# Sparse attention and a mixture of experts on one core: wider local turns, a strided unit moved ahead, more filler products, one store on another queue

## The chip, the cores and the metric

One Trainium2 chip, one NeuronCore of it. The metric is the device time of one execution in microseconds; lower is better. The engines are TensorE (PE for products, PEld for the load of their stationary operand), VectorE (DVE), ScalarE (ACT), GpSimd (POOL) and SyncE (SP), whose queue issues most transfers.

## The reference

Four batches, eight heads, 576 positions, 64 channels, float32. Heads 0 to 3 attend to the last 32 positions ("local"), heads 4 to 7 to earlier positions of the same remainder modulo 32 ("strided"). The result, 2304 rows of 512, goes through a mixture of 8 experts with one expert for each row.

```python
mask_local = (rel >= 0) & (rel < stride)                       # stride = 32
mask_strided = (rel >= 0) & (pos[None, :] % stride == pos[:, None] % stride)
scores = np.where(masks, scale * q @ k.T, -1e9)
attn_out = softmax(scores) @ v
x = attn_out.transpose(0, 2, 1, 3).reshape(B * S, H * D)
logits = x @ w_gate
expert_idx = np.argmax(logits, axis=1)
# rows go to their expert while it has room (576 rows)
out[i] = gate_w[i] * (np.maximum(x[i] @ w1[e], 0) @ w2[e])
```

## The kernel before

Attention is cut into 16 strided units (`z`) and 9 local ones (`l`). A strided unit is a pair of heads of one batch and half of its position groups; a local unit is 256 rows of the result for the four local heads. Each unit goes through five stages: A turns q and k (they come with positions on the partitions and are needed with channels there), B makes scores, C turns the weights after exp, D multiplies by v, E turns the result for the gate and stores it to `x_dram`. The string `SEQ` is the order of the units, and a loop over its places i runs C(i), A(i+3), B(i+2), E(i-1), exp, D(i): so each engine's program interleaves five units. A turn is a TensorE product with the identity `ident` into one of three PSUM buffers of `ps_t` (tag "t"), from where ScalarE copies it out.

For local units stage A is `l_a(c, nm)`, once for k and once for q of each of 8 head pairs c. `la_target` spreads these 16 calls over the places ahead of the unit that needs them; for batch 0 they start at place `LS`. GpSimd reorders their source first (`l_r`). `fill(t)` is a product of the all-ones tile `hot` (bf16) written into a PSUM tile that the next turn overwrites: it computes nothing that is used. `warm(n)` is n such products of 512 columns.

Loads are issued on SyncE's queue by `put_to` and `put_more`, in the order of their need, a fixed look-ahead in front of the place (`LOOK`), and as far as buffers are free. The queue works in order, and the stores to `x_dram` of stage E go through it as well. The first of all are q and k of the first head pair (`load_z(0, 2)`), then v (`load_zv`) into the buffers `VZ`, whose rows 32 to 63 VectorE sets to zero beforehand.

Behind the last unit, VectorE works out ranks and the first expert; SyncE reads the first expert's number and loads its first weights (`load_w`, twice 512 KB); GpSimd gathers that expert's rows out of `x_dram` (`gather_tile`, three tiles, indices `idx`), TensorE turns them (`x_steps`), and `experts` runs all eight experts (line 1063 is the first product, lines 1052 to 1054 the others). The gathers need every row of `x_dram`, so they wait for the last store too: that of unit `vv == 8` in `l_e`.

Of the kernel before, what the change touches and what calls it, by code (L numbers as in the profile page):

```python
# [9 lines left out]
F32 = mybir.dt.float32  # L10
# [10 lines left out]
STRIDE = 32  # L21
FL = "abgi"
LOOK = 8
SEQ = "zzzzlzzlzzlzzlzzlzzlzzlll"
WARM2 = 4
WA = 2
WB = 6
# [5 lines left out]
NZ = 3  # L33
NL = 3
NV = 3
LS = 3
WARM = 14
SETS = (
# [7 lines left out]
def bc(ap, axis, n):  # L46

    a = ap.unsqueeze(axis)
    shape = list(a.shape)
    shape[axis] = n  # L50
    return a.to_broadcast(shape)
# [3 lines left out]
def kernel(  # L55
# [10 lines left out]
    nc = tc.nc  # L66
# [25 lines left out]
    ident = const.tile([128, 128], F32, name="ident")  # L92
# [22 lines left out]
    def gather_tile(idx, r, xg_p):  # L115
        t = xg_p.tile([128, DM], F32, tag="xg", name="xg")
        nc.gpsimd.indirect_dma_start(  # L117
            out=t[:r], out_offset=None, in_=x_dram[:, :],
            in_offset=bass.IndirectOffsetOnAxis(ap=idx[:r], axis=0),
        )  # L120
        return t, r


    with ExitStack() as p1:
# [5 lines left out]
        ps_t = p1.enter_context(tc.tile_pool(name="ps_t", bufs=3, space=PSUM))  # L130
# [20 lines left out]
        def fill(t):  # L151

            w = t.shape[1]
            nc.tensor.matmul(t, lhsT=hot, rhs=bc(hot[:, 0:w // 4], 1, 4), start=True, stop=True)

        V0S = [cp.tile([128, 16, 65], F32, name=f"v0s{i}") for i in range(NV)]
        VZ = [cp.tile([128, 16, 64], F32, name=f"vz{i}") for i in range(2)]
        V0L = [cp.tile([128, 18, 65], F32, name=f"v0l{i}") for i in range(4)]
        KTL = [cp.tile([128, 32 + S], F32, name=f"ktl{i}") for i in range(4)]
        QTL = [cp.tile([128, S], F32, name=f"qtl{i}") for i in range(4)]  # L160
# [30 lines left out]
        def load_zv(c):  # L191
            b, pair = divmod(c, 2)
            h0 = 4 + 2 * pair
            for h in range(2):
                nc.sync.dma_start(
                    out=VZ[c % 2][64 * h:64 * h + 36],
                    in_=v[b, h0 + h].rearrange("(m g) d -> m g d", g=16),
                )

        def copy_zv(c):  # L200
            nc.gpsimd.tensor_copy(V0S[c % NV][0:100, :, 0:64], VZ[c % 2][0:100])

        def copy_lv(c):
            vt = V0L[c % 4]
            for h in range(2):
                nc.gpsimd.tensor_copy(vt[64 * h:64 * h + 32, 1:18, 0:64], vt[64 * h + 32:64 * h + 64, 0:17, 0:64])  # L206
# [9 lines left out]
        def load_lv(c):  # L216
            b, pair = divmod(c, 2)
            h0 = 2 * pair
            vt = V0L[c % 4]
            for h in range(2):  # L220
# [2 lines left out]
        load_z(0, 2)  # L223
        for i in range(NV):
            nc.gpsimd.memset(V0S[i][:, :, 64], 1.0)
        for i in range(2):
            nc.vector.memset(VZ[i][32:64], 0.0)
        for t in PS:
            nc.gpsimd.memset(t, 0.0)
        for i in range(4):  # L230
            nc.gpsimd.memset(KTL[i][:, 0:32], 0.0)
            nc.gpsimd.memset(V0L[i][:, :, 64], 1.0)
            for h in range(2):
                nc.gpsimd.memset(V0L[i][64 * h:64 * h + 32, 0, 0:64], 0.0)

# [72 lines left out]
        def zid(u):  # L308
            c, gh = divmod(u, 2)
            b, pair = divmod(c, 2)  # L310
            return b, pair, gh, c

        def z_a(u):
            b, pair, gh, c = zid(u)
            for src, nm in ((zk[c], "k"), (zq[c], "q")):
                t = ps_t.tile([128, 4, 72], F32, tag="t", name="tq")
                if nm == "q":
                    fill(t.rearrange("p a b -> p (a b)"))
                for i in range(4):
                    g, h = divmod(i, 2)  # L320
                    g = 4 * gh + 2 * g
                    nc.tensor.transpose(t[:, i, :], src[:, h, g:g + 2, :].rearrange("p g d -> p (g d)"), ident[:72, :72])
                st = wk.tile([128, 4, 72], F32, tag=nm + "t", name=nm + "t")
                nc.scalar.copy(st, t)
                (kts if nm == "k" else qts)[u] = st
# [86 lines left out]
        def l_a(c, nm):  # L412
            src = lr.pop((c, nm))
            dst = QTL[c % 4] if nm == "q" else KTL[c % 4][:, 32:32 + S]
            for p0, p1 in ((0, 64), (64, 96)):
                n = p1 - p0
                t = ps_t.tile([128, 6, n], F32, tag="t", name="tl")
                if p0 == 0:
                    fill(t.rearrange("p a b -> p (a b)"))
                for g in range(6):  # L420
                    nc.tensor.transpose(t[:, g, :], src[p0:p1, g].rearrange("p h d -> p (h d)"), ident[p0:p1, p0:p1])
                nc.scalar.copy(dst[:, 6 * p0:6 * p1].rearrange("d (p g) -> d p g", g=6), t.rearrange("d g p -> d p g"))

        def l_b(vv):
            s = ps_s.tile([128, 2, 512], F32, tag="s", name="sl")
# [24 lines left out]
        def l_c(vv):  # L450
            p = Pl.pop(vv)
            t = ps_t.tile([128, 4, 128], F32, tag="t", name="tpl")
            for i in range(4):
                nc.tensor.transpose(t[:, i, :], p[:, i].rearrange("p h k -> p (h k)"), ident)
            pt = wk.tile([128, 4, 128], F32, tag="pt", name="ptl", bufs=2)
            nc.scalar.copy(pt, t)
            PTl[vv] = pt

        def l_d(vv):
            pt = PTl.pop(vv)  # L460
            o = ps_o.tile([128, 2, 512], F32, tag="o", name="ol")
            for t in range(2):
                for pair in range(2):
                    i = 2 * t + pair
                    for c in range(4):
                        b, blk = divmod(4 * (2 * vv + t) + c, 18)
                        n = (2 * b + pair) % 4
                        for h in range(2):
                            nc.tensor.matmul(
                                o[32 * c:32 * c + 32, h, 65 * i:65 * i + 65],  # L470
                                lhsT=pt[64 * h:64 * h + 64, i, 32 * c:32 * c + 32],
                                rhs=V0L[n][64 * h:64 * h + 64, blk, :],
                                start=True, stop=True,
# [8 lines left out]

        def l_e(vv):
            x = Xl.pop(vv)
            nc.sync.dma_start(
                out=x_dram[256 * vv:256 * vv + 256, 0:256].rearrange("(t p) c -> p t c", p=128),
                in_=x.rearrange("p (t a) h d -> p t (a h d)", t=2),
            )
            t = ps_t.tile([128, 4, 128], F32, tag="t", name="txl")
            for i in range(4):  # L490
                nc.tensor.transpose(t[:, i, :], x[:, i].rearrange("p h d -> p (h d)"), ident)
            xt = wk.tile([128, 4, 128], F32, tag="xtl", name="xtl", bufs=4)
            nc.scalar.copy(xt, t)
            xtl[vv] = xt
# [202 lines left out]
        zu, lu = list(range(16)), list(range(9))  # L697
        for c in SEQ:
            seq.append(("z", zu.pop(0)) if c == "z" else ("l", lu.pop(0)))
        at = {x: i for i, x in enumerate(seq)}  # L700
        n = len(seq)
# [3 lines left out]
        def last_l(b):  # L705
            return (18 * (b + 1) - 1) // 8

        def emit_la(m):
            while la_done[0] < m:
                c, part = divmod(la_done[0], 2)  # L710
                assert c < 4 or done["B", "l"] > last_l((c - 4) // 2)
                put_to("lr", c)
                l_a(c, "kq"[part])
                la_done[0] += 1
# [4 lines left out]
        def la_target(i):  # L719
# [3 lines left out]
            for b in range(B):  # L723
                s0 = first[b - 1] + 1 if b == 1 else (at["l", last_l(b - 2)] + 2 if b > 1 else LS)
                s1 = first[b]
# [56 lines left out]
        def stage(st, i):  # L782
            if not 0 <= i < n:
                return
            kind, u = seq[i]
            if st == "A":
                if kind == "z":
                    put_to("zq", u // 2)
                    z_a(u)
                emit_la(l_need(u) if kind == "l" else la_target(i))  # L790
            elif st == "B":
                (z_b if kind == "z" else l_b)(u)
            elif st == "C":
                (z_c if kind == "z" else l_c)(u)
            elif st == "D":
                if kind == "z":
                    put_to("zc", u // 2)
                else:
                    put_to("lc", 2 * min((8 * u + 7) // 18, B - 1) + 1)
                (z_d if kind == "z" else l_d)(u)  # L800
            elif st == "E":
                (z_e if kind == "z" else l_e)(u)
            done[st, kind] += 1
# [82 lines left out]
        g0 = [gather_tile(idx[0], 128, xg_p)]  # L886
# [112 lines left out]
    with ExitStack() as p2:  # L999
        p0 = p2.enter_context(ExitStack())  # L1000
# [181 lines left out]
        t = pools["ps_w"].tile([128, 512], F32, tag="w", name="warm2")  # L1182
# [133 lines left out]
```

## Time and profile before

| what | value |
|---|---|
| median of 3 runs | 420.32 us (419.13 to 426.94) |
| profiled execution, its own time | 416.89 us |
| its span | 415.1 us |
| TensorE busy (products) | 376.1 us, 91% |
| mean granted TensorE clock | 0.884 |
| attention, from the first turn to the last unit's scores for the gate | 6.6 to about 153 us |
| first product of the experts | 174.47 us |

A granted clock of 1.00 in the profile is 2.4 GHz and one of 0.50 is 1.2 GHz. The timeline names an instruction, its start, its length, and in brackets how long its engine stood idle before it and what ended that.

### The profile page before, as it was taken

Reading aid. Unit: us, or ns where it says so; the run is one execution under the profiler, and the core shown is the slowest. Engines: PE = TensorE matmul, PEld = TensorE weight load, DVE = VectorE, ACT = ScalarE, POOL = GpSimd, SP = SyncE. Lnnn points to the kernel's source line nnn. Section 1 sums busy time; section 2 is a strip of 40 time slices with the busy share of each in tenths; the row PEclk is TensorE's granted clock in tenths of the full one; section 3 lists DMA queues with packets and bytes.
Section 4 is the critical chain, followed back from the end, with each engine's and each line's share of the span. In section 5 each row is a group of like instructions: output and inputs, shape, how many; then the busy total and the mean of one; then the engine's idle time right before and its main releaser. Section 6 shows DMA issues by size and latency. Waiting matters only on the chain. (4 is left out here: it accounts for less than half of the span.)

```text
span 415.1 us, 11988 instructions
## 1 busy us (share of the span) xinstructions
PE 376.1 (91%) x5067; PEld 335.9 (81%) x5068; DVE 219.3 (53%) x472; ACT 167.8 (40%) x324; POOL 113.9 (27%) x164
## 2 busy tenths in 40 slices
PE   6899987989999783699999999999999999999990
PEld 3678866868777551499999999999999899989980
DVE  7153345523736664362756655656566475675630
ACT  3334444433455321242544434435453355454520
POOL 4464511152040002043603403404405015021300
PEclk9555699665989896589999999999999999999996
DMA  5998955731232126549945536548647557476101
GB/s 144 214 179 194 216 172 137 161 105 32 63 79 59 32 70 198 193 18 209 350 160 188 170 129 217 164 118 259 212 159 221 173 170 241 122 239 203 47 3 52
DMA packets 56169, 62.99 MB, mean 152 GB/s; under 512 B 15989, under 2 KB 42933, under 8 KB 56106
## 3 DMA queue, kind: packets, MB, share of 16 engines
q1 hardware_dynamic: 52218, 52.47, 44.9%
q0 software_dynamic: 3888, 9.66, 8.2%
q8 instruction: 42, 0.69, 0.7%
q14 instruction: 21, 0.17, 0.1%
HBM read 52.67 MB, written 9.60 MB: 150 GB/s over the span
## 5 line engine op out<-in xcount | busy, mean ns | idle before, releaser
L1052 PE MATMUL ph<-xh,w1h 128*128 128x280 f32 (+5 forms) x252 | 78.8, 313 | 0.0
L1054 PE MATMUL ph<-xh,w1l 128*128 128x280 f32 (+5 forms) x252 | 75.5, 300 | 0.0
L1053 PE MATMUL ph<-xl,w1h 128*128 128x280 f32 (+5 forms) x252 | 75.4, 299 | 0.0
L1069 ACT ACTIVATE hh<-ph 128x280 fp32r<-128x280 f32 (+5 forms) x64 | 26.8, 419 | 87.6 <-PE ph L1054 80.4
L1053 PE MATMUL y<-hl,w2h 128*128 128x280 f32 (+4 forms) x192 | 58.9, 307 | 1.0 <-DVE hl L1070 0.8
L1054 PE MATMUL y<-hh,w2l 128*128 128x280 f32 (+4 forms) x192 | 58.5, 305 | 0.0
L1052 PE MATMUL y<-hh,w2h 128*128 128x280 f32 (+4 forms) x192 | 58.5, 305 | 0.0
L1098 POOL DMA_INDIRECT out_dram<-yo,routing x22 | 21.8, 990 | 130.4 <-DVE yo L1123 100.6
L1070 DVE SCALAR_TENSOR_TENSOR hl<-ph,hh 128x280 fp32r<-128x280 f32 (+5 forms) x64 | 29.7, 464 | 41.9 <-ACT hh L1069 38.0
L1052 PEld LDWEIGHTS ph<-xh,w1h 128*128 128x128 f32 x252 | 47.8, 190 | 0.5
L1053 PEld LDWEIGHTS ph<-xl,w1h 128*128 128x128 f32 x252 | 47.8, 190 | 0.2
L1054 PEld LDWEIGHTS ph<-xh,w1l 128*128 128x128 f32 x252 | 47.6, 189 | 0.0
L1032 DVE TENSOR_TENSOR w1l<-w1r,w1h 128x1024 fp32r<-128x1024 f32 x31 | 38.0, 1225 | 16.8 <-ACT w1h L1031 13.3
L1032 DVE TENSOR_TENSOR w2l<-w2r,w2h 128x1024 fp32r<-128x1024 f32 x32 | 39.0, 1219 | 2.0 <-issue 1.2
L1053 PEld LDWEIGHTS y<-hl,w2h 128*128 128x128 f32 x192 | 36.1, 188 | 1.9 <-DVE hl L1070 1.9
L1052 PEld LDWEIGHTS y<-hh,w2h 128*128 128x128 f32 x192 | 36.1, 188 | 0.1
L1054 PEld LDWEIGHTS y<-hh,w2l 128*128 128x128 f32 x192 | 36.1, 188 | 0.0
L1031 ACT CAST w2h<-w2r 128x1024 fp32r<-128x1024 f32 x32 | 33.6, 1050 | 4.2 <-PE y L1053 1.3
L1031 ACT CAST w1h<-w1r 128x1024 fp32r<-128x1024 f32 x31 | 32.3, 1041 | 3.0 <-DMA w1r<-in_moe_w_dram 3.0
L117 POOL DMA_INDIRECT xg<-x_dram,routing x19 | 20.9, 1102 | 28.1 <-PE px L1042 12.2
L1135 POOL DMA_INDIRECT gt<-g_dram,routing x22 | 23.7, 1076 | 16.8 <-PE ph L1054 10.4
L206 POOL COPY v0l<-v0l 32x1088 f32<-32x1088 f32 x16 | 17.4, 1089 | 34.4 <-DMA v0l<-in_v_dram 33.7
(207 smaller groups left out, 651.3 us busy)
## 6 DMA issues: line engine op xcount, KB each, us to landing
w1r<-in_moe_w_dram SPq DMA_DIRECT2D x32, 512.0 KB
w2r<-in_moe_w_dram SPq DMA_DIRECT2D x32, 512.0 KB
vz<-in_v_dram SPq DMA_DIRECT2D x16, 144.0 KB
lk<-in_k_dram SPq DMA_DIRECT2D x8, 288.0 KB
lq<-in_q_dram SPq DMA_DIRECT2D x8, 288.0 KB
v0l<-in_v_dram SPq DMA_DIRECT2D x16, 144.0 KB
x_dram<-xz SPq DMA_DIRECT2D x16, 144.0 KB
x_dram<-xl SPq DMA_DIRECT2D x9, 256.0 KB
```

The lines of the kernel that those rows point to most:

```text
L117: nc.gpsimd.indirect_dma_start(out=t[:r], out_offset=None, in_=x_dram[:, :], in_offset=bass.IndirectOffsetOnAxis(ap=idx[:r], axis=0),)
L206: nc.gpsimd.tensor_copy(vt[64 * h:64 * h + 32, 1:18, 0:64], vt[64 * h + 32:64 * h + 64, 0:17, 0:64])
L1031: nc.scalar.copy(hi, t)
L1032: nc.vector.tensor_tensor(lo, t, hi.bitcast(F32), op=ALU.subtract)
L1052: nc.tensor.matmul(o, lhsT=wh, rhs=xh, start=first, stop=False)
L1053: nc.tensor.matmul(o, lhsT=wh, rhs=xl, start=False, stop=False)
L1054: nc.tensor.matmul(o, lhsT=wl, rhs=xh, start=False, stop=last)
L1069: nc.scalar.activation(hh, o, AF.Relu)
L1070: nc.vector.scalar_tensor_tensor(hl, o, 0.0, hh.bitcast(F32), op0=ALU.max, op1=ALU.subtract)
L1098: s = nc.gpsimd.indirect_dma_start(out=out[:, :], out_offset=bass.IndirectOffsetOnAxis(ap=idx, axis=0), in_=o, in_offset=None, bounds_chec ...
L1135: nc.gpsimd.indirect_dma_start(out=t[:r], out_offset=None, in_=g_dram[:, :], in_offset=bass.IndirectOffsetOnAxis(ap=idx_r(i)(j)[:r], axis=0),)
```

## The change

Five edits. (1) In `l_a`, two groups of rows (0 to 63, 64 to 95) with six transposes each become two groups of three position groups with all 96 rows: 12 transposes become 6, the two copies become equally long, and the one filler product in front has 288 columns in place of 384. (2) `SEQ` has a fifth strided unit ahead of the first local one (and one less near the end); `LS` goes from 3 to 4, so that the turns of batch 0 still begin one place ahead. (3) More filler products: three more in front of each of the k and the q turns of strided units 1 to 5 (30 products of 288 columns), and one of 512 columns in front of the turns in `l_c` and `l_e` of each of the nine local units (18). (4) The two clears of `VZ` are written further up. (5) The store of the last local unit goes through GpSimd's queue.

```diff
-SEQ = "zzzzlzzlzzlzzlzzlzzlzzlll"
+SEQ = "zzzzzlzzlzzlzzlzzlzzlzlll"
-LS = 3
+LS = 4
...
         VZ = [cp.tile([128, 16, 64], F32, name=f"vz{i}") for i in range(2)]
+        for i in range(2):
+            nc.vector.memset(VZ[i][32:64], 0.0)
...
-        for i in range(2):
-            nc.vector.memset(VZ[i][32:64], 0.0)
         for t in PS:
...
                 t = ps_t.tile([128, 4, 72], F32, tag="t", name="tq")
-                if nm == "q":
+                for _ in range((nm == "q") + 3 * (0 < u < 6)):
                     fill(t.rearrange("p a b -> p (a b)"))
...
-            for p0, p1 in ((0, 64), (64, 96)):
-                n = p1 - p0
-                t = ps_t.tile([128, 6, n], F32, tag="t", name="tl")
-                if p0 == 0:
+            for g0 in (0, 3):
+                t = ps_t.tile([128, 3, 96], F32, tag="t", name="tl")
+                if g0 == 0:
                     fill(t.rearrange("p a b -> p (a b)"))
-                for g in range(6):
-                    nc.tensor.transpose(t[:, g, :], src[p0:p1, g].rearrange("p h d -> p (h d)"), ident[p0:p1, p0:p1])
-                nc.scalar.copy(dst[:, 6 * p0:6 * p1].rearrange("d (p g) -> d p g", g=6), t.rearrange("d g p -> d p g"))
+                for g in range(3):
+                    nc.tensor.transpose(t[:, g, :], src[:, g0 + g].rearrange("p h d -> p (h d)"), ident[:96, :96])
+                nc.scalar.copy(dst.rearrange("d (p g) -> d p g", g=6)[:, :, g0:g0 + 3], t.rearrange("d g p -> d p g"))
...
             t = ps_t.tile([128, 4, 128], F32, tag="t", name="tpl")
+            fill(t.rearrange("p a b -> p (a b)"))
...
-            nc.sync.dma_start(
+            (nc.gpsimd if vv == 8 else nc.sync).dma_start(
                 out=x_dram[256 * vv:256 * vv + 256, 0:256].rearrange("(t p) c -> p t c", p=128),
...
             t = ps_t.tile([128, 4, 128], F32, tag="t", name="txl")
+            fill(t.rearrange("p a b -> p (a b)"))
```

TensorE before, at the first local turns; they stand behind the turns of strided unit 3 (`tq` is a strided turn or its filler, `tl` a local one, `sz` strided scores):

```order
L322 MATMUL tq<-ident,zq 128x72 x4
L154 LDWEIGHTS hot
L154 MATMUL tl<-hot 128x384
L421 MATMUL tl<-ident,rk 128x64 x6
L421 MATMUL tl<-ident,rk 128x32 x6
L154 LDWEIGHTS hot
L154 MATMUL tl<-hot 128x384
L421 MATMUL tl<-ident,rq 128x64 x6
L421 MATMUL tl<-ident,rq 128x32 x6
L332 LDWEIGHTS identb
```

TensorE in the changed kernel, at the same local turns, which now stand behind strided unit 4:

```order
L154 LDWEIGHTS hot
L154 MATMUL tq<-hot 128x288
L322 MATMUL tq<-ident,zq 128x72 x4
L154 LDWEIGHTS hot
L154 MATMUL tl<-hot 128x288
L420 MATMUL tl<-ident,rk 128x96 x6
L154 LDWEIGHTS hot
L154 MATMUL tl<-hot 128x288
L420 MATMUL tl<-ident,rq 128x96 x6
L332 LDWEIGHTS identb
```

The local turns have half as many transposes and come one strided unit later; of the pair of filler rows at the top three more stand ahead of it, and three ahead of that unit's k turns.

VectorE at the program's start, before (-) and now (+):

```order
 L142 MEMSET nb 128x1
-L173 CAST io<-it 128x128
-L174 CAST pp<-ip 128x1
-L227 MEMSET vz_113 32x1024
-L227 MEMSET vz_114 32x1024
+L159 MEMSET vz_113 32x1024
+L159 MEMSET vz_114 32x1024
+L175 CAST io<-it 128x128
+L176 CAST pp<-ip 128x1
 L250 TENSOR_SCALAR zi<-zi 128x36
```

The clears of `VZ` moved in front of two casts that read what GpSimd writes; everything else keeps its place.

SyncE's queue before, behind the last unit but one (the TENSOR_LOAD rows read an expert's number into a register):

```order
L485 DMA x_dram<-xl 128x2x256 x2
L873 TENSOR_LOAD order_75
L873 ISA x2
L104 ISA
L104 DMA w1r<-in_moe_w_dram 128x4x256
L109 ISA
L109 DMA w2r<-in_moe_w_dram 128x2x512
L485 DMA x_dram<-xl 128x2x256
L1179 TENSOR_LOAD order
```

GpSimd's queue in the changed kernel, at the same place:

```order
L208 COPY v0l_120<-v0l_120 32x17x64 x2
L485 DMA x_dram<-xl 128x2x256
L117 DMA xg<-x_dram,idx_76 128x512
L117 DMA xg<-x_dram,idx_77 128x512
L117 DMA xg<-x_dram,idx_78 128x512
```

The last store left its place behind the two weight loads on SyncE's queue and stands directly ahead of the gathers on GpSimd's.

## Rows read from the trace of the kernel before

**Rows 1.** The page: span; TensorE's clock in 40 slices
```profile
span 415.1 us, 11988 instructions
...
PEclk9555699665989896589999999999999999999996
```

**Rows 2.** Windows: length, busy PE PEld DVE ACT POOL, PEclk, DMA share, GB/s
```profile
12.00:49.40 37.40, 36.52 (x575) 29.81 (x576) 14.13 (x36) 14.13 (x39) 21.23 (x46) 0.50 0.96 196
49.40:73.30 23.90, 19.54 (x630) 15.68 (x629) 9.68 (x27) 11.21 (x28) 4.65 (x6) 1.00 0.60 164
73.30:151.00 77.70, 71.55 (x2086) 57.60 (x2085) 40.60 (x121) 32.95 (x83) 13.91 (x14) 0.80 0.30 77
151.00:174.50 23.50, 11.89 (x120) 6.54 (x120) 10.86 (x76) 3.56 (x7) 3.06 (x3) 0.66 0.55 180
```

**Rows 3.** Timeline of SyncE's queue and VectorE at the start
```profile
2.07 0.39 SPq L186 DMA_DIRECT2D zq<-in_q_dram  x1
5.21 0.72 SPq L195 DMA_DIRECT2D vz<-in_v_dram  x2
...
4.27 0.91 DVE L227 MEMSET vz<- 32x1024 f32 x1 [0.25 <-issue]
```

**Rows 4.** Timeline of TensorE at the third strided unit
```profile
11.39 0.44 PE L322 MATMUL tq<-ident,zk 72*128 72x72 f32 x4 [2.69 <-DMA zk<-in_k_dram]
...
12.88 0.74 PE L322 MATMUL tq<-ident,zq 72*128 72x72 f32 x4 [0.93 <-DMA zq<-in_q_dram]
```

**Rows 5.** Timeline of TensorE at a clock of 0.50
```profile
37.95 0.45 PE L154 MATMUL tq<-hot 128*128 128x288 bf16 x1
38.19 0.69 PE L322 MATMUL tq<-ident,zq 72*128 72x72 f32 x4
...
39.13 1.67 PE L421 MATMUL tl<-ident,rk 64*128 64x64 f32 x12
40.73 0.48 PE L332 MATMUL sz<-mz,identb 128*100 128x144 bf16 x2
```

**Rows 6.** Timeline of TensorE at a clock of 1.00
```profile
56.09 0.51 PE L354 MATMUL tp<-ident,ps 100*128 100x100 f32 x4
56.44 0.42 PE L322 MATMUL tq<-ident,zk 72*128 72x72 f32 x4
56.69 0.29 PE L154 MATMUL tq<-hot 128*128 128x288 bf16 x1
56.82 0.41 PE L322 MATMUL tq<-ident,zq 72*128 72x72 f32 x4
...
57.49 1.07 PE L421 MATMUL tl<-ident,rk 64*128 64x64 f32 x12
58.49 0.33 PE L332 MATMUL sz<-mz,identb 128*100 128x144 bf16 x2
```

**Rows 7.** Timeline of TensorE just ahead of 73.3 us
```profile
72.36 0.28 PE L322 MATMUL tq<-ident,zq 72*128 72x72 f32 x1 [1.68 <-issue]
```

**Rows 8.** Timeline behind the last local unit, all engines
```profile
150.41 0.69 DVE L480 TENSOR_TENSOR xl<-ol,sml 128x512 f32<-128x512 f32 x1
...
154.38 0.39 SPq L109 DMA_DIRECT2D w2r<-in_moe_w_dram  x1
154.59 0.15 DVE L645 TENSOR_REDUCE idx<-ix 128x1 uint32<-128x8 f32 x1
154.87 1.08 SPq L485 DMA_DIRECT2D x_dram<-xl  x1
...
158.00 2.95 PE L149 MATMUL warm<-hot 128*128 128x512 bf16 x8
...
161.60 1.16 POOL L117 DMA_INDIRECT xg<-x_dram,idx  x1 [41.40 <-DVE t L681]
...
166.49 1.11 PE L1163 MATMUL px<-ident,xg 128*128 128x128 f32 x4 [5.55 <-DMA xg<-x_dram,idx]
...
174.47 1.51 PE L1063 MATMUL ph<-xh,w1h 128*128 128x352 f32 x4 [0.77 <-ACT xh L1164]
```

## The prediction, on record before the result

> **What bounds the kernel now.** I read the page's strips first, then busy time by stage, then TensorE's timeline, which says why that engine is slow where it is. TensorE is near full in most slices, but the granted clock is not: in the first 40% of the span its digits are mostly 5 to 9, and from about 180 us on they are 9s [rows 1]. Everything before that is attention and the hand-over, and all five edits lie there; the experts behind it (231 us at full clock) are not touched, so I let them move as a block.
>
> By stage [rows 2]: from 12.0 to 49.4 us TensorE is busy 36.5 of 37.4 us at a clock of 0.50, half of what it can have. From 49.4 to 73.3 it is granted 1.00 and is busy 19.5 of 23.9. From 73.3 to 151 the mean is 0.80, which at two levels (0.50 and 1.00) means 40% of that time, 31 us, at half. No other engine is above 60% busy in any of these. So attention is TensorE's own program, stretched by its clock. The transfers are the next thing: in the half-clock stretch the DMA engines are busy 0.96 of the time at 196 GB/s, later 0.60 and 0.30.
>
> Two more places wait. At the start the third strided unit's turns stand idle 2.69 and 0.93 us for their data [rows 4], and the clock falls to half right behind that. Behind attention, TensorE waits for the first gather: it starts at 161.60, although its index stood at 154.74 [rows 8]. The page puts that wait down to VectorE's line 681, but the gather needs no result of that line. What it does need is the last store: it was issued at 154.87 to 155.95, behind 1 MB of weights on the same queue.
>
> **The change part by part.** The sum goes by the profiled execution, 416.9 us.
>
> *The clears moved up.* The v load into the buffers was issued at 5.21, directly behind the clear that ends at 5.18, while the load ahead of it left at 2.07 to 2.46 [rows 3]. With the clears first on VectorE it can go at about 2.6, and all later loads 2.6 us earlier. The two idle times of [rows 4], 3.6 us, shrink by that: -3.2 (I keep 0.4 for transfers that now queue tighter). VectorE pays nothing: the casts only swap places with the clears, and the chain of masks behind both starts at the same time.
>
> *Fillers ahead of strided units 1 to 5.* 30 products of 288 columns. At full clock one takes 0.13 us (56.69 to 56.82 [rows 6]), at half 0.24 (37.95 to 38.19 [rows 5]): +3.9, or +7.2 if the clock stays at half. Where the turn behind them waits for data they are hidden; I claim none of that. What they are worth is the clock. No row shows the start with them, so I bound it. If the stretch of 37.4 us keeps the half clock: 0. If it is granted 1.00 throughout: the same piece of program costs, half against full, 0.24 against 0.13 for a filler and 1.60 against 1.00 for a local turn (39.13 to 40.73 and 57.49 to 58.49), so 0.54 and 0.63 of the time. I take 0.60 of 37.4, a gain of 15.0. I take the upper end, -15.0: what stands between the start, granted 1.00 [rows 1], and the half clock is the idle time of [rows 4], which the moved clears remove; and from 49.4 us on the same mix of stages ran at 1.00 with one filler a unit [rows 2], so units with seven should not fare worse.
>
> The Trainium skill speaks against that: "TensorE: Matmul & The Clock Gate", Part 4, says that the full clock does not engage for transposes, since they don't count as busy in the same way. In this trace stages with many transposes did run at 1.00 once the clock was there [rows 6], which leaves the rule open here; by the rule the sum would be that of the first rival.
>
> *Wider local turns.* A turn of k or q costs 1.00 us at full clock for 12 transposes. Six transposes with 96 moving columns lie between those of 72 (four in 0.25 us, 56.44 to 56.69, so 0.063 each) and those of 100 (0.35, so 0.088 each, 56.09 to 56.44 [rows 6]). I take 0.088, being next to 100: 0.53 for six, a gain of 0.475, times 16: -7.6. Ends: 0.063 gives -10; if the width cost as much as two of the old ones each (0.083 times 2), 0. ScalarE still copies the same elements in two steps.
>
> *18 fillers of 512 columns in the local units.* 512/288 of 0.13 us is 0.23: +4.1 at full clock, and up to +7.5 at half. In return the later stretch holds more bf16 products and fewer transposes. Its 31 us at half are worth 12.4 if all of them went (times 0.40), nothing if none. Part of them follow idle times that stay: 1.68 us without any releaser (the bracket says issue) stand right ahead of the fall at 73.3 [rows 7]. So I take a third: -4.0.
>
> *One more strided unit ahead, turns of batch 0 one place later.* No work is added. It shifts the first local unit by one strided unit and gives its data and GpSimd's reordering that time. Cost nothing while the loads keep ahead.
>
> *New waits.* A TensorE at twice the speed asks for its data sooner. At 196 GB/s and 0.96 busy [rows 2] the old pace of 37.4 us brought 7.3 MB; were every byte needed within the stretch, it could not get shorter, and the waits would eat the whole 15.0. But the loads are issued up to eight places ahead, and behind [rows 4] TensorE stood idle nowhere in the stretch (busy 36.5 of 37.4 us, and the 0.93 there is the rest). I take +3.5, nearer to nothing than to 15. Idle times of the kind in [rows 7] come with fast runs of small products; a faster engine meets more of them: +2.0.
>
> *The last store on GpSimd's queue.* Its data stands at 151.10 (150.41 + 0.69), GpSimd has nothing else to do, and neither SyncE's wait for the expert's number nor 1 MB of weights is ahead any more. Issue by GpSimd as long as a gather's, 1.2 us, and a transfer that no row isolates, 2 to 3 us, end at 154.3 to 155.3. The first gather then goes at about 155.3 in place of 161.60. TensorE behind it is held by its own filler products up to 160.95 [rows 8], so the first turn moves from 166.49 to 161 (5.5 us) and the first expert product, which hangs on the third gather, by about 6: -6.0. Bounds: 0 (the gathers do wait for line 681), and -8.5 (the third gather meets emptier DMA engines too). Nothing queues behind that store but the gathers, which need it anyway.
>
> On issue the Trainium skill, "DMA: Bandwidth & Descriptors", Specifications, gives GpSimd's path about 1 us to the first byte and SyncE's 0.6: by it the store costs an estimated 0.4 us more, and the term would be -5.6.
>
> Sum: -3.2 + 3.9 - 15.0 - 7.6 + 4.1 - 4.0 + 3.5 + 2.0 - 6.0 = -22.3, so 394.6 from 416.9. The median of the three runs is 3.4 above the profiled one. I add nothing for that and say 395: the runs differ where the clock falls, and there is less of that if I am right.
>
> **The rivals.**
> First: *the start stays at half clock.* For it: 37 us in a row at 0.50 with TensorE 98% busy, so a full engine alone did not bring the clock back [rows 2]. Against: the new fillers, and no idle time ahead of them. Then the 15.0 go and the 30 fillers cost 7.2; the new waits go too. -3.2 + 7.2 - 7.6 + 4.1 - 4.0 - 6.0 = -9.5, about 407. Chance 0.15.
> Second: *the transfers take the place of the clock.* The clock rises but TensorE waits for data, as DMA is at 0.96. If the waits reach the upper end, 12 in place of 3.5, the sum is -13.8, about 403. Against: in the stretch at 1.00 the share was 0.60, and TensorE idle for only 4.4 of 23.9 us, whatever the cause. Chance 0.17.
> Third, slower: *the later stretch loses its clock.* The filler in a local turn shrinks from 384 to 288 columns, and each idle time can drop the clock. Were 73 to 151 us wholly at half, its 46.6 us at full become 46.6/0.60, +31, without the -4.0: with the first rival's other terms -5.5 + 31 = +25, about 442. It turns slower than before where some 8 of those 47 us fall to half on top of a cold start. For it: the clock is unsteady there already. Against: the 18 new fillers. Chance 0.04.
> Fourth: *nothing measurable*, cold start and the gathers waiting for VectorE: -9.5 + 6.0 = -3.5, about 413. Chance 0.06.
>
> **How the numbers follow.** Forecast as above 0.58, between 380 and 400, the low end by the turns at -10, the tail at -8.5, a later stretch that recovers two thirds (-8) and no new waits. The four rivals hold 0.42. The range from 379 to 408 takes in the forecast, the second and most of the first rival, and leaves out some 0.18. A measurement of this kernel tells about 2% (8.4 us) from no change, so faster means below 411.9: forecast, first and second rival, less a tenth for their spread: 0.86 faster, 0.10 same, 0.04 slower.
>
> **What would show it.** Right: a clock digit of 9 in the slices from 10 to 40 us; no idle ahead of the third strided unit's turns; local turns of half a microsecond; the first gather some 4 us behind the last local unit's final VectorE step, not 10.5; the v load issued at 2.6. Wrong: 5s in those slices (first rival); idle TensorE put down to transfers between 15 and 50 us (second); more 5s after 73 us than before (third); a first gather that still follows VectorE's line 681 (fourth).

## The result and the profile after

The changed kernel takes 386.32 us in the median of four runs (383.59 to 388.24), the kernel before on the same chip 420.85 (419.13 to 426.94). The ratio is 0.919, with a 95% interval from 0.910 to 0.928: faster. The profiled execution took 388.24 us, span 386.4, so 28.7 us of span went away. The forecast was 395 from a sum of -22.3. The total is inside the range; where it came from is only partly as said. The profiled execution is the slowest of the four: by the medians 34.5 us went away, where 25 were forecast.

The page of the changed kernel, against [rows 1], with the line for the queue that brings TensorE's instructions:

```profile
span 386.4 us, 11889 instructions
...
PEclk9996585899999989999999999999999999999996
...
q8 instruction: 41, 0.67, 0.7%
```

The 9s now reach to about 29 us, then come 6, 5, 8, 5 and 8, and from 77 us on it is 9s nearly everywhere. So a stretch at half clock is still there; it starts later and is shorter. By windows, against [rows 2] (length, busy PE with its instructions, PEclk, DMA share, GB/s):

```profile
12.00:32.40 20.40, 18.86 (x460) 1.00 0.95 199
32.40:49.50 17.10, 12.82 (x263) 0.50 0.92 186
49.50:73.30 23.80, 20.01 (x520) 0.71 0.66 180
73.30:133.25 59.95, 53.25 (x1933) 1.00 0.34 86
```

The last local unit's final VectorE step ends at 133.25 us in place of 151.10 [rows 8]. That is where I end "attention" below. The start, against [rows 3] to [rows 6], by the timeline of all engines:

```profile
1.98 0.91 DVE L159 MEMSET vz<- 32x1024 f32 x1 [0.28 <-issue]
2.92 0.72 SPq L197 DMA_DIRECT2D vz<-in_v_dram  x2
...
9.67 0.42 PE L322 MATMUL tq<-ident,zk 72*128 72x72 f32 x4
9.93 0.66 PE L154 MATMUL tq<-hot 128*128 128x288 bf16 x4
10.88 0.47 PE L322 MATMUL tq<-ident,zq 72*128 72x72 f32 x4 [0.30 <-DMA zq<-in_q_dram]
...
16.73 0.29 PE L154 MATMUL tl<-hot 128*128 128x288 bf16 x1
16.86 0.66 PE L420 MATMUL tl<-ident,rk 96*128 96x96 f32 x6
17.44 0.28 PE L154 MATMUL tl<-hot 128*128 128x288 bf16 x1
```

The v load leaves at 2.92 (5.21 before), the third unit's turns wait 0.30 us (3.62 before), and a local turn takes 0.58 us here (16.86 to 17.44), 0.49 at 29.44. Then come the waits that took the old ones' place:

```profile
31.66 1.04 POOL L203 COPY v0s<-vz 100x1024 f32<-100x1024 f32 x1 [7.67 <-DMA vz<-in_v_dram]
32.76 1.13 PE L370 MATMUL oz<-v0s,ptz 36*64 36x65 f32 x32 [1.62 <-POOL v0s L203]
...
33.88 1.74 SPq L394 DMA_DIRECT2D x_dram<-xz  x2
39.26 0.69 DVE L381 TENSOR_TENSOR xz<-oz,smz 100x512 f32<-100x512 f32 x1 [4.88 <-DMA x_dram<-xz]
40.09 0.90 PE L389 MATMUL tx<-ident,xz 100*128 100x100 f32 x4 [3.92 <-DVE xz L381]
...
53.28 0.45 PE L370 MATMUL oz<-v0s,ptz 36*64 36x65 f32 x15
56.64 0.70 PE L370 MATMUL oz<-v0s,ptz 36*36 36x65 f32 x17 [2.92 <-issue]
```

First TensorE waits for a v load and GpSimd's copy of it. Then VectorE waits for one of the two strided result buffers (`xz`) whose store was issued only at 33.88, on the queue where the loads stand, and TensorE waits for VectorE. The last wait lies in the middle of 32 equal products (15 and 17 of them) and names nobody. The clock falls to half at 32.42 and 56.31, at the first and the third of these waits. Behind attention, against [rows 8]:

```profile
132.56 0.69 DVE L480 TENSOR_TENSOR xl<-ol,sml 128x512 f32<-128x512 f32 x1
133.57 0.91 POOL L485 DMA_DIRECT2D x_dram<-xl  x1 [24.03 <-DVE xl L480]
137.22 0.15 DVE L646 TENSOR_REDUCE idx<-ix 128x1 uint32<-128x8 f32 x1
138.24 1.13 POOL L117 DMA_INDIRECT xg<-x_dram,idx  x1 [3.76 <-DVE r_oa L585]
143.83 1.67 PE L1164 MATMUL px<-ident,xg 128*128 128x128 f32 x8 [0.59 <-DMA xg<-x_dram,idx]
148.84 0.88 PE L1064 MATMUL ph<-xh,w1h 128*128 128x352 f32 x4 [2.04 <-ACT w2h L1032]
```

The first gather starts 4.99 us behind the last unit (10.50 before) and 0.87 behind its index, so it is VectorE's index that comes last now, no longer the store. The first expert product stands 15.59 us behind the last unit, 23.38 before. It now waits 2.04 us for ScalarE's cast of the weights.

Attention can be split without a remainder: at each granted clock the time in which TensorE is busy, and its idle time. Busy time at half clock weighs 0.60 at full, the forecast's own ratio; "clock" is the other 0.40 of it. From 6 us to the end of attention, in the profiled executions (E1 to E11 are the experiments below, numbered as they were made, without a ninth; A and B the changed kernel again on the other two chips):

| kernel | end of attention | busy at half | busy at full | work (full + 0.60 x half) | clock (0.40 x half) | idle |
|---|---|---|---|---|---|---|
| before | 151.1 | 67.3 | 63.5 | 103.9 | 26.9 | 14.2 |
| changed | 133.3 | 25.2 | 85.4 | 100.5 | 10.1 | 16.6 |
| changed, A | 132.5 | 21.0 | 89.0 | 101.6 | 8.4 | 16.6 |
| changed, B | 132.4 | 11.0 | 95.1 | 101.7 | 4.4 | 20.3 |
| E1, no early fillers | 132.3 | 27.1 | 82.3 | 98.5 | 10.8 | 16.9 |
| E2, old local turns | 136.9 | 23.9 | 98.5 | 112.9 | 9.6 | 8.4 |
| E4, no late fillers | 132.3 | 18.7 | 88.1 | 99.3 | 7.5 | 19.5 |
| E8, third result buffer | 127.6 | 19.7 | 89.0 | 100.9 | 7.9 | 12.8 |
| E7, fillers and clears of the start alone | 133.1 | 20.5 | 95.7 | 108.0 | 8.2 | 11.0 |
| E10, turns and store alone | 129.7 | 21.6 | 83.0 | 96.0 | 8.7 | 19.0 |

So 28.7 us of span are 17.8 in attention (work -3.4, clock -16.8, idle +2.4), 7.8 in the hand-over, and 3.0 in the experts' block, 237.6 us in place of 240.6. That last piece I leave out of the account: it lies between 237.3 and 240.8 in all profiles of this study. Of the 3.0, some 1.9 are clock as well: in the kernel before the block starts at 174.47, and the clock is back only at 179.15.

The same busy time at half clock can be split by the place in the program. Fillers and local turns left out, TensorE has 4792 products in every one of these kernels; the first 557 of them are through at 49.5 us in the kernel before, the first 1139 at 73.3, where its clock changed [rows 2]. (With the new order of units the same count is not quite the same units.)

| kernel | busy at half, first piece | second piece | third piece |
|---|---|---|---|
| before | 36.7 | 0.0 | 30.7 |
| changed | 3.1 | 22.1 | 0.0 |
| changed, A | 3.0 | 14.8 | 3.3 |
| changed, B | 0.0 | 7.5 | 3.4 |
| E1, no early fillers | 7.0 | 20.1 | 0.0 |
| E4, no late fillers | 0.0 | 10.9 | 7.8 |
| E7, start alone | 3.4 | 13.7 | 3.4 |
| E10, turns and store alone | 5.7 | 10.6 | 5.4 |

Each row of the two tables is one execution. The kernel before has one profile, and so this split once; the mean clock of its other executions, 0.86 to 0.92, says that it varies there too.

### The profile page after: what moved, and what is told of

The parts are those of the page before. It is cut to its first block, busy times and chain, and to the rows that moved or that the text cites. A ratio compares the mean times of both kernels' runs of the same rounds, so it can differ in the third digit from the quotient of the medians.

```text
span 386.4 us, 11889 instructions
## 1 busy us (share of the span) xinstructions
PE 351.2 (91%) x5019; PEld 319.9 (83%) x5020; DVE 214.8 (56%) x472; ACT 167.7 (43%) x324; POOL 116.1 (30%) x165
## 5 line engine op out<-in xcount | busy, mean ns | idle before, releaser
L1070 ACT ACTIVATE hh<-ph 128x280 fp32r<-128x280 f32 (+5 forms) x64 | 26.9, 420 | 87.3 <-PE ph L1055 84.8
L1033 DVE TENSOR_TENSOR w1l<-w1r,w1h 128x1024 fp32r<-128x1024 f32 x31 | 38.0, 1225 | 17.7 <-ACT w1h L1032 16.6
L117 POOL DMA_INDIRECT xg<-x_dram,routing x19 | 22.3, 1175 | 23.7 <-PE px L1043 12.2
```

The source lines that it names most:

```text
L117: nc.gpsimd.indirect_dma_start(out=t[:r], out_offset=None, in_=x_dram[:, :], in_offset=bass.IndirectOffsetOnAxis(ap=idx[:r], axis=0),)
L1033: nc.vector.tensor_tensor(lo, t, hi.bitcast(F32), op=ALU.subtract)
L1070: nc.scalar.activation(hh, o, AF.Relu)
```

## The experiments

Kernels of one chip share their runs of the kernel before: 416.95 us (409.35 to 418.56) for E1 to E4, 417.56 (412.04 to 428.86) for E5, E6, E8 and A, 420.17 (416.35 to 424.47) for the rest. The changed kernel was not run on the chip of E1 to E4. These four are held against its 386 to 390 us on the other three chips, so that a difference of less than some 4 us can't be told there.

**E1. Without the early fillers.**

```diff
-                for _ in range((nm == "q") + 3 * (0 < u < 6)):
+                for _ in range(int(nm == "q")):
```

> The changed kernel (386.3 us) without the three extra fillers ahead of each turn of strided units 1 to 5. Theory (the fillers hold the clock): the 20.4 us from 12.0 to 32.4, all at 1.00, lose 3.9 us of fillers and run at 0.50 instead, 16.5/0.60 = 27.5, so 7 us later and a total of about 393 (389 to 400), with 5s in the page's slices from 15 to 35 us. Rival (the moved clears alone keep the clock, fillers only cost): 1.00 still granted up to 30 us and 3.9 us less, about 382.

Measured: 387.05 us (386.11 to 389.49), 0.939 of before (0.926 to 0.952). Neither side: the 30 products cost 2 to 3 us of work (98.5 against 100.5 to 101.7 in the table), and the total doesn't move measurably without them. In this run the third unit's turns wait 0.89 and 0.76 us for their data, the clock fell behind that, at 12.76 us, and was back at 19.59, with one filler a unit. So without the fillers the fall at the start comes again, but it is short, and what the forecast credited them with does not hang on them.

**E2. With the old local turns** (two groups of rows, 12 transposes, filler of 384 columns).

```diff
-            for g0 in (0, 3):
-                t = ps_t.tile([128, 3, 96], F32, tag="t", name="tl")
...
+            for p0, p1 in ((0, 64), (64, 96)):
+                n = p1 - p0
+                t = ps_t.tile([128, 6, n], F32, tag="t", name="tl")
...
```

> The changed kernel with the local turns of before (12 transposes of 64 and 32 rows, filler of 384 columns). Theory: each of the 16 turns costs 1.00 in place of 0.49 us at full clock, 8 us in all, so about 394 to 395; if the longer turns also bring the half clock back after 70 us, up to 405. Rival (TensorE has slack for them, the transfers set the pace): under 2 us, 386 to 388.

Measured: 401.22 us (392.26 to 404.73), 0.976 (0.961 to 0.991), 15 us more. The profiled execution is the fastest of these four, 392.26, 6 us more; the ratio is that of the three others, which are 13 to 18 us more. The work of the profiled one is 112.9 against 100.5 to 101.7, 11 to 12 us of it for the turns. The others have a lower mean clock (0.925 to 0.936, against 0.955); no profile shows where they lose it.

**E3. The last store back on SyncE's queue.**

```diff
-            (nc.gpsimd if vv == 8 else nc.sync).dma_start(
+            nc.sync.dma_start(
```

> The changed kernel with the last local store back on SyncE's queue. Theory (the store behind the weights held the gathers): the first gather again 10.5 us behind the last VectorE step of the last local unit in place of 5.0, the first expert product some 8 us later and its start at half clock for 3 us more: 394 to 397. Rival (the gathers wait for VectorE's ranks, as the page's releaser says): first gather unmoved, 386 to 388.

Measured: 397.6 us (395.74 to 398.46), 0.964 (0.952 to 0.976), 11 us more than the changed kernel's 386.32. Its timeline behind attention:

```profile
131.27 0.69 DVE L480 TENSOR_TENSOR xl<-ol,sml 128x512 f32<-128x512 f32 x1
135.66 0.15 DVE L646 TENSOR_REDUCE idx<-ix 128x1 uint32<-128x8 f32 x1
135.84 0.39 SPq L109 DMA_DIRECT2D w2r<-in_moe_w_dram  x1
136.33 0.41 SPq L485 DMA_DIRECT2D x_dram<-xl  x1
142.78 1.16 POOL L117 DMA_INDIRECT xg<-x_dram,idx  x1 [33.99 <-DVE t L682]
155.04 0.88 PE L1064 MATMUL ph<-xh,w1h 128*128 128x352 f32 x4 [0.77 <-ACT xh L1165]
```

The index stands at 135.81, as early as in the changed kernel, and the gather goes 7.0 us later, 6.0 behind the end of the store's issue at 136.74. On GpSimd's queue it went 3.8 us behind it, and there the index came last. The bracket names line 682 here as it named 681 before, and the edit touches neither: the store was the cause, as read ahead of the change. In the three profiles with the store on SyncE's queue the first expert product stands 23.0 to 23.4 us behind attention, in the eleven with the other 13.4 to 16.6.

**E4. Without the late fillers** (in `l_c` and `l_e`).

```diff
-            fill(t.rearrange("p a b -> p (a b)"))
...
-            fill(t.rearrange("p a b -> p (a b)"))
```

> The changed kernel without the 18 fillers of 512 columns in the local units. Theory (they keep the clock at 1.00 from 70 us to the end of attention): 4 us less work, but half clock back for 15 to 30 us of it, which costs 6 to 12: 388 to 394, with 5s in the page's slices after 70 us. Rival (the shorter turns alone keep the clock): 1.00 as now and 4 us less, about 382.

Measured: 387.17 us (384.51 to 390.42), 0.933 (0.918 to 0.948). They cost 1 to 2 us of work (99.3 against 100.5 to 101.7), and the time is the same without them within what can be told. In the third piece of the program this run was busy at half clock for 7.8 us, the changed kernel for 0, 3.3 and 3.4 us in its three profiles. That they hold the clock there is not shown: E7 and E10, which don't have them either, have 3.4 and 5.4 us there, and E11, which has them, 12.6.

**A. The changed kernel again**, on the chip of the next three.

> The changed kernel once more, beside the others on the same chip, as their yardstick: 386 as before, or a few us less if this chip also runs the kernel before faster than 420.

Measured: 390.05 us (388.89 to 391.08), 0.939 (0.931 to 0.946).

**E5. The clears of `VZ` back in their old place.**

```diff
-        for i in range(2):
-            nc.vector.memset(VZ[i][32:64], 0.0)
...
+        for i in range(2):
+            nc.vector.memset(VZ[i][32:64], 0.0)
```

> The changed kernel with the two clears where they stood before. Theory of the prediction (the loads come 2.6 us earlier, and the idle time that drops the clock goes): TensorE again idle for 1 to 2.7 us ahead of the third strided unit's turns, and the clock at half soon after 12 us in spite of the fillers: 3 to 8 us slower. Rival (what the first experiments suggest: the pace up to 40 us is set by the transfers, not by the clock): the whole pattern moves by the 2.6 us of the later loads, 388 to 389 beside the changed kernel's 386.

Measured: 387.89 us (387.01 to 390.86), 0.935 (0.926 to 0.943): no difference. The v load leaves at 5.22 again, but the third unit's turns wait only 0.47 and 0.79 us, because the fillers ahead of them fill the rest.

**E6. The old order of units.**

```diff
-SEQ = "zzzzzlzzlzzlzzlzzlzzlzlll"
+SEQ = "zzzzlzzlzzlzzlzzlzzlzzlll"
-LS = 4
+LS = 3
```

> The changed kernel with the old order of units (four strided units ahead of the first local one) and LS of 3. Theory (the order costs and brings nothing by itself): within 2 us of the changed kernel. Rival (the order is what lets TensorE run at full clock through the time in which data is short, as strided units need less of it): local turns meet their loads and GpSimd's reordering, idle TensorE between 12 and 30 us, clock at half there, 6 to 12 us slower.

Measured: 386.06 us (384.8 to 389.76), 0.931 (0.921 to 0.940), against A's 0.939 (0.931 to 0.946): not told apart, though three of its four runs lie below all of A's. The wait for `xz` is not in its trace, others are.

**E8. A third buffer for the strided result** (`xz`), so that VectorE need not wait for the store.

```diff
-                xcur[0] = wk.tile([100, 2, 4, 2, 64], F32, tag="x", name="xz", bufs=2)
+                xcur[0] = wk.tile([100, 2, 4, 2, 64], F32, tag="x", name="xz", bufs=3)
```

> The changed kernel with a third buffer for the strided results (xz). In its trace TensorE stands idle for 3.92 us at 36 us because VectorE waits for a store of the buffer two head pairs back, which sits on SyncE's queue behind loads. Theory (that wait ended the gain of the full clock): the idle time goes, and 4 to 6 us with it, 380 to 383. Rival (the transfers as a whole set the pace there): a wait for v or k data of about the same length takes its place, 385 to 387.

Measured: 384.13 us (382.2 to 387.21), 0.925 (0.915 to 0.935). All four runs lie below A's four (388.89 to 391.08) on the same chip, the median by 5.9 us; but E6, without this edit, lies 4.0 below A. Its timeline at the place of the old wait:

```profile
33.93 0.68 PE L370 MATMUL oz<-v0s,ptz 36*64 36x65 f32 x32 [2.41 <-POOL v0s L203]
35.13 0.69 DVE L381 TENSOR_TENSOR xz<-oz,smz 100x512 f32<-100x512 f32 x1
35.35 1.86 SPq L394 DMA_DIRECT2D x_dram<-xz  x2
```

VectorE's step at line 381 has no idle time any more (4.88 us in the changed kernel), and idle in attention falls from A's 16.6 to 12.8 us. The wait for v stays.

**E7. The kernel before with the early fillers and the moved clears alone.**

```diff
+        for i in range(2):
+            nc.vector.memset(VZ[i][32:64], 0.0)
...
-                if nm == "q":
+                for _ in range((nm == "q") + 3 * (0 < u < 6)):
```

> The kernel before with only the two edits of the start: the VectorE clears of the two v buffers moved up, and three extra filler products ahead of each of the first strided turns. Theory (the prediction's): these two are what holds the early clock, so the stretch from 12 to 49 us runs mostly at full clock and the kernel takes about 403 us where the one before takes 417 to 420 (15 gained on the clock, 3 on the clears, 4 paid for the fillers). Rival: the two alone hold nothing that lasts, because transfers or waits open the same holes; then the time stays within 3 us of the kernel before, 414 to 420, and the stretch falls to half clock again before 30 us.

Measured: 400.33 us (395.98 to 408.75), 0.953 (0.945 to 0.960): 20 us less than before, and the rival falls, although the clock does drop once before 30 us:

```profile
6.00:21.90 15.90, 15.43 (x296) 1.00 1.02 220
21.95:25.30 3.35, 3.35 (x46) 0.50 1.05 158
25.35:45.80 20.45, 16.54 (x514) 1.00 0.85 203
```

Against before, the table has +4.1 of work (forecast +3.9), -18.7 of clock and -3.2 of idle. In the first piece of the program the clock gives -13.3, where -15.0 was said: taken alone, the start does what the prediction said of it. The rest of the -18.7 lies further on, +5.5 in the second piece and -10.9 in the third, where the prediction had put the late fillers' gain. Nor are the -3.2 of idle the clears' alone: with both edits the third unit's turns wait 0.28 us (3.62 before), with the clears and no fillers 1.65 (E1), with the fillers and no clears 1.26 (E5).

**E10. The kernel before with the wider turns and the store on GpSimd's queue alone**: old order, old clears, no extra fillers.

```diff
-            for p0, p1 in ((0, 64), (64, 96)):
...
+            for g0 in (0, 3):
+                t = ps_t.tile([128, 3, 96], F32, tag="t", name="tl")
...
-            nc.sync.dma_start(
+            (nc.gpsimd if vv == 8 else nc.sync).dma_start(
```

> The kernel before with only the 96-row local turns and the last row store on GpSimd's queue; the order, the clears and all extra fillers stay as before. Undoing clears, early fillers, late fillers and order one at a time each left the time where it was. Theory: the turns and the store are the whole gain, 386 to 392 us. Rival: the other four stand in for one another, each enough to hold the clock when one is missing; with all four gone the long stretch at half clock from 12 to 49 us is back and the time is 398 to 405.

Measured: 384.51 us (383.68 to 390.88), 0.918 (0.912 to 0.923), the whole gain with two edits of five; B, on the same chip, has 0.929 (0.923 to 0.935), and three of E10's four runs lie below all of B's. The store acts only behind attention. Its windows (as above) and TensorE's timeline at the third strided unit:

```profile
13.00:16.40 3.40, 3.40 (x22) 0.50 1.01 243
16.40:33.40 17.00, 14.91 (x471) 1.00 0.99 202
33.50:40.30 6.80, 4.57 (x51) 0.50 0.82 189
```

```profile
10.55 0.44 PE L322 MATMUL tq<-ident,zk 72*128 72x72 f32 x4 [1.38 <-DMA zk<-in_k_dram]
11.93 0.47 PE L322 MATMUL tq<-ident,zq 72*128 72x72 f32 x4 [0.82 <-DMA zq<-in_q_dram]
...
15.22 1.16 PE L420 MATMUL tl<-ident,rk 96*128 96x96 f32 x6
16.42 0.66 PE L420 MATMUL tl<-ident,rq 96*128 96x96 f32 x6
```

As before, the turns wait for their data (2.2 us in this run, 3.6 in [rows 4]), and the clock falls right behind, at 13.0 us. But it is back at 16.4, where before it stayed at half until 49.4 [rows 2]: the six transposes at 16.42 take 0.66 us, those at 15.22 took 1.16. The first local turns, at 14.98 us here, are where the two programs begin to differ; that the clock is back during them is seen, why it is back is not.

**E11. The changed kernel with the old order and the third buffer together.**

> The changed kernel with the order of before (four strided units ahead of the first local one) and three result buffers for the strided units in place of two. Theory: the third buffer takes away the wait of VectorE for a store that is stuck on SyncE's queue, and the old order does the same by another way, so both together give what the buffer alone gave, 382 to 386. Rival: they take away different waits and add up, 378 to 381.

Measured: 389.41 us (382.99 to 393.14), 0.921 (0.912 to 0.930). Neither side: it can't be told from B.

**B. The changed kernel again**, on the chip of E7, E10 and E11.

> The changed kernel as it is, for comparison on the same chip: 386 to 390 us by both theories.

Measured: 388.13 us (387.94 to 392.48), 0.929 (0.923 to 0.935).

## Why the prediction was right in sum, and where it was not

| term | forecast | measured | from |
|---|---|---|---|
| early fillers, late fillers, turns (work) | +3.9 +4.1 -7.6 = +0.4 | -3.4 | table, changed against before |
| clock, early and late | -15.0 -4.0 = -19.0 | -13.4 +8.8 -12.3 = -16.8 (rounded) | busy at half by piece, times 0.40 |
| idle: clears, new data waits, issue | -3.2 +3.5 +2.0 = +2.3 | -3.3 +5.5 +0.2 = +2.4 | idle times of [rows 4] and those of 1 us or more; sum from the table |
| hand-over | -6.0 | -7.8 | first expert product behind the last unit |
| experts | 0 | -3.0 | some -1.9 clock, the rest not attributed |
| sum | -22.3 | -28.6 | spans: -28.7 |

*What bounds the kernel.* Right: attention was TensorE's program at half clock. With 25.2 in place of 67.3 us of busy time at half, it is 16.8 us shorter for that alone.

*The clock.* The sum was nearly right, and partly by luck; the cause was not right. By place, the first piece gave -13.4 where -15.0 was said. The last gave -12.3 where -4.0 was said, a third of the 12.4 that the prediction itself had as the upper end, and not by the late fillers (E4, E7 and E10 have 7.8, 3.4 and 5.4 us of half clock there without them, where the kernel before has 30.7). The second piece, at full clock before, lost 8.8: the forecast counted the time of the new waits and put at nothing the clock that falls at them. In A and B that loss is 5.9 and 3.0, and the last piece gives -10.9.

The prediction said that the fillers and the moved clears bring the clock back and gave the turns their own time alone. E7 shows that the start's edits do it without the turns (-18.7), E10 that the turns do it without the start's edits (-18.3, with 2.2 of the 3.6 us of idle time and the fall behind it still there). Each saves nearly the same 18 us, and they can be saved only once. That fits that each of the four small edits could be undone without a loss (E1, E4, E5, E6), which looks as if none mattered, and it is why the sum came out: it counted the clock once and put it down to one of two edits that each bring it. The step "the clock rises because the idle time of [rows 4] goes" fails as well: in E10 most of it stays. What wider turns and more fillers have in common that ends a spell at half clock is not settled; no run varies it by itself. The first rival's 37 us in a row are gone in every variant with either edit. The Trainium skill's rule in "TensorE: Matmul & The Clock Gate", Part 4, that transposes don't bring the full clock, is not borne out as that rival needed it: E10, with no filler added, has 17 us at 1.00 in which 72 of its 471 products are transposes; a stretch of transposes alone is in no run.

*Wider turns.* A little mis-sized: -7.6 against -7.9 (work of E10 less that of before) to -12 (E2's 112.9 against 100.5 to 101.7). A turn behaves as said, 0.49 to 0.58 us against 1.00, 6.7 to 8.2 us for 16. What was left out is its filler, 384 columns before and 288 after. From its start to that of the turn are 0.13 us (16.73 to 16.86); with the filler of before it is 0.26 at full clock in E7 (19.40 to 19.66), so 16 x 0.13 = 2.1 us more. What E2 has above that is open.

*Fillers.* They cost less than said: 2.0 to 3.1 for 3.9 early, 1.2 to 2.3 for 4.1 late. The total doesn't show that they return it in this kernel.

*New waits.* The second rival was there in part. TensorE waits 1.62 and 3.92 us between 31 and 40 us for data and for a store among the loads, 5.5 where the forecast had 3.5. The idle times of 1 us or more marked "issue" went from three with 4.8 us to two with 5.1, where +2.0 was said; A has three with 6.3, B six with 8.5. That the idle times add up to the forecast's sum is luck. It did not see the place: not the loads' rate alone, but a store on the same queue that holds a result buffer. In E8 that wait is gone, and its runs are about 6 us below A's. E11 does not show the gain again and E6 has 4 of the 6 us without the third buffer, so what the wait is worth is open.

*Order of units.* Costed at nothing; E6 shows no cost of undoing it.

*The store.* Right in mechanism. The first gather moved by 5.5 us (6.3 said: the index now comes last), the first turn behind it by 4.8 (5.5 said). The first expert product gained 7.8 in place of 6, toward the bound of -8.5: from the first gather to it are 10.6 us in place of 12.9, and E3, at 12.3, agrees. The emptier DMA engines that the bound names are not shown. What the traces show is the clock: it stands at half through that piece in the kernel before (158.67 to 179.15) and through most of it in E3 (144.26 to 154.5), in the changed kernel only from 141.64 to 145.06.

*The experts.* The prediction let them move as a block of 231 us at full clock. The block is 240.6 us [rows 8], its first 4.7 at half clock.

## What to carry to other kernels

Where a gain comes from the clock, two edits can each bring the whole of it, and together no more than one of them. Undoing one at a time then shows that nothing matters; try each alone on the old kernel as well. A transfer that a dependent chain waits for belongs on a queue where nothing stands ahead of it, even when its bytes are unchanged; and a bracket that names an instruction long done is best tested by moving the transfer.

## What the runs showed of the hardware

TensorE's idle times marked "issue" look like waits for its own program; no run varies the program's length alone, so this rests on when they end. Queue q8, which the page calls "instruction", brings 41 packets of 16 KB, 0.67 MB, in the changed kernel; spread over the 5019 products and 5020 weight loads of its page, that is 67 bytes each. In all fourteen profiles, of the idle times of 1 us or more that are marked so on PE between 10 and 137 us (52 of them, 1.0 to 3.9 us), every one ends 1.24 to 1.68 us behind the end of one of these packets. Of the 20 other idle times of that length in the same stretches, which the profile puts down to a transfer or an engine, one does. There are 22 to 27 packets in each stretch, so such places make up less than a tenth of it. The one at 53.7 to 56.6 us in the changed kernel has its packet from 54.2 to 55.3; the one of [rows 7], ending at 72.36, from 69.8 to 71.1. They stop the engine in the middle of a row of equal products, and the clock fell at several of them (at 56.31 in the changed kernel, at 33.48 in E10 within one of 3.65 us that ends at 35.73). If so, fewer and wider products also load less program: the turns alone leave out 96 transposes with their weight loads. The Trainium skill, "Runtime: NRT & Kernel Launch", Instruction fetch mechanics, says that instructions come in such blocks of 16 KiB and that crossing into the next is mostly hidden. That agrees with most of the packets here: of the 22 to 27 in each stretch, 2 to 6 go with an idle time of 1 us or more.
